# The inverse product over 32 places with a row's high and low part stacked in one operand, and the correction added a stage later

## The chip, the cores and the metric

One NeuronCore of a Trainium2 chip runs the whole kernel in one launch. The metric is device time in microseconds (us), the median over several executions.

## The reference, cut to what matters

```
x: (1, 2048, 576)    w_r, w_i: (2048, 289)    w_gate, w_up: (576, 4608)    w_down: (4608, 576)
xn = layernorm(x)                                     # over the 576
spectral = irfft2(rfft2(xn) * (w_r + 1j * w_i))       # over rows (2048) and columns (576)
glu = (sigmoid(xn @ w_gate) * (xn @ w_up)) @ w_down
out = x + spectral + glu
```

Everything is float32.

## The kernel before, in words

**Precision.** A product of float32 matrices is made on TensorE from rounded parts. Each operand is split into a high part (a copy on ScalarE that rounds) and a low part (the operand minus its high part, on VectorE), and three products are added: high by high, low by high, high by low.

**The gated unit.** The hidden dimension of 4608 is cut into 36 blocks, and the 2048 rows into two halves of two blocks each. A block of hidden columns is a unit. In most units the 2 × 2 block products are made by a scheme of seven products instead of eight (`unit`, with `prod` at L659: seven matmuls of 512 columns on a product bank, called pA, pB or pE). The down product is also done by seven rounds (`seven`, matmuls at L1016, 12 of 288 columns into a pair of banks called ps), and its last part plainly (`down`, L809, po). The units of the second pass over the rows take about 2.8 us per step, seven steps each. Weights for these units lie in one buffer `w_6086`, which SP refills slot by slot after TensorE has read a slot.

**The spectral part.** The 2048-point transform along the rows is split into 64 × 32. Phase 1 does the transform over the columns and the forward product over the 64 places, phase 2 does the forward product over the 32 places, the multiplication with the filter and the inverse product over the 32 places, phase 3 does the inverse product over the 64 places and the inverse column transform. Each phase is a generator per chunk of rows (16 chunks, `phase1b`, `phase2`, `phase3`), and every `yield` ends a chunk of work. After each step of the gated unit `aside` advances every live generator by one chunk. `U1`, `U2`, `U3` (L51) give each phase its first step and the steps between two generators, so the spectral work is spread under the gated unit by these numbers. A scheduler then orders the instructions of each engine when the program is built, and an engine runs them in that order. All but a few DMAs are issued by SP in one queue, in order.

**Phase 2 before (L496 to L541).** Per i: x2 (580 KB) and the filter piece ri (580 KB, two buffers) are loaded. Two products pb0 and pb1 (L513, two matmuls of 290 columns each) use stacked operands: the high part of the data in 64 partitions, the low part in the other 64, and main and correction come out in two halves of the bank and are added on VectorE (L517). s is turned with four copies on ScalarE (sw, L522), multiplied with the filter (L523 to L527), and z, which holds two sets of 32 complex places in its 128 partitions (real above imaginary, 64 rows a set), is split into zh (ScalarE, L530) and zl (VectorE, L532). The inverse product pc (L538) is six matmuls: for each of two column groups high, low and correction, with a 128 × 128 block-diagonal constant. ScalarE copies pc to u (L540), and one DMA (L541, 290 KB) writes u to the scratch array `sc2` in HBM.

**Phase 3 before (L544 to L612).** Per t: u (290 KB) and constants ai are loaded, u is split into uh (L559) and ul (L560), the product py follows (L566, six matmuls), its result is copied to y (L569) and the remainder columns split into rp (L572, L573). pz (L579, L582) are six transposes into one pair of banks, z3h, z3r and z3l (L587 to L589) are their split copies, pe (L599) twelve matmuls, and L601 to L610 add the result to `fin` or `acc`. All pairs of banks (pb, pc, ps, py, pz, pe, po) come from one pool of two pairs.

Of the kernel before, what the change touches and what calls it, by code (L numbers as in the profile page):

```python
# [167 lines left out]
def spectral_glu_kernel(ctx: ExitStack, tc: tile.TileContext, x, xt, xg, ri, w_in, w_down, out):  # L168
# [327 lines left out]
    def phase2(i):  # L496
        pool, bm, zz = R["pool"], R["bm"], R["zz"]
        kl = 2 * i
# [10 lines left out]
        for h, o in enumerate((s, c)):  # L509
            yield  # L510
            pb = pair(f"pb{i}_{h}")
            for j in range(2):
                nc.tensor.matmul(pb[:, j, :NQ], bm[:, h, :], x2[:, h, j, :], start=True, stop=True)  # L513
# [16 lines left out]
        nc.scalar.activation(zh, z, AF.Copy)  # L530
        yield
        nc.vector.tensor_tensor(zl, z, f32(zh), op=OP.subtract)  # L532
        yield
        yield
        pc = pair(f"pc{i}")
        for j in range(2):
            for n, (k, m) in enumerate(((2, zh), (2, zl), (3, zh))):
                nc.tensor.matmul(pc[:, j, :NQ], bm[:, k, :], m[:, j, :], start=n == 0, stop=n == 2)  # L538
# [1 line left out]
        nc.scalar.activation(u, pc[:, :, :NQ], AF.Copy)  # L540
        nc.sync.dma_start(sc2.rearrange("(p kl) n -> p kl n", kl=N2)[:, kl:kl + 2], u)  # L541

    def phase3(t):
        pool, di, dr = R["pool"], R["di"], R["dr"]  # L544
# [15 lines left out]
        nc.vector.tensor_tensor(ul, u, f32(uh), op=OP.subtract)  # L560
# [3 lines left out]
        for sl in range(2):  # L564
            for n, (h, m) in enumerate(((0, uh), (0, ul), (1, uh))):
                nc.tensor.matmul(py[:, sl, :NQ], ai[:, sl, h, :], m[:, sl, :], start=n == 0, stop=n == 2)  # L566
# [985 lines left out]
```

## Time and profile before

| | us |
|---|---|
| median of 3 executions | 1357.94 (1357.67 to 1358.01) |
| profiled execution | 1357.6 |
| its span, first to last instruction | 1355.8 |
| TensorE busy | 1344.5 (99%) |
| VectorE busy | 1078.5 (80%) |
| ScalarE busy | 815.3 (60%) |
| granted TensorE clock | 1.00 throughout |

The profile names PE for TensorE's matmuls, PEld for its weight loads, DVE for VectorE, ACT for ScalarE, SP for SyncE, and SPq for its DMA queue. `out<-in` are the names of tiles; a line such as L538 is that line of the kernel. Busy shares are means over stages with different limits, and the chain of work that ended last says which engine's work sets the end.

### The profile page before, as it was taken

The page shows a single profiled execution, that of the slowest core. Times are in us where ns is not written, and L with a number is a line of the kernel's source. Part 1 is how long each engine was busy: PE and PEld are TensorE (multiplying, and loading weights), DVE is VectorE, ACT ScalarE, POOL GpSimd, SP SyncE. Part 2 cuts the span into 40 slices and gives each one's busy share as a digit, 9 for nine tenths or more (in the row PEclk, how much of TensorE's full clock was granted, in tenths as well). Part 3 has the DMA queues.
Part 4 walks back from the last instruction along what each step waited for, and adds up shares of the span by engine and source line. Part 5 has one row for each costly group of instructions (what it writes and reads, how often), then busy time and mean ns, then how long its engine had stood idle before and what let it go on. Part 6 is the DMA issues. An engine that isn't in the chain of part 4 may idle for free.

```text
span 1355.8 us, 20569 instructions
## 1 busy us (share of the span) xinstructions
PE 1344.5 (99%) x7589; PEld 1193.7 (88%) x7589; DVE 1078.5 (80%) x1624; ACT 815.3 (60%) x1266; POOL 3.3 (0%) x5
## 2 busy tenths in 40 slices
PE   8999999999999999999999999999999999999998
PEld 6888888888888888889899999988888889889997
DVE  7898998889898897888477777758878856777786
ACT  6667777776767677778355554546767634444432
POOL 0000000000000000000000000000000000000000
PEclk9999999999999999999999999999999999999999
DMA  6468888778787877688899887798999787776543
GB/s 235 187 256 324 313 314 309 285 287 330 283 326 290 321 290 285 265 313 293 287 336 294 259 263 251 209 310 308 307 304 313 244 280 252 237 228 207 187 135 88
DMA packets 151828, 366.17 MB, mean 270 GB/s; under 512 B 14240, under 2 KB 54704, under 8 KB 147120
## 3 DMA queue, kind: packets, MB, share of 16 engines
q1 hardware_dynamic: 150736, 363.55, 77.4%
q8 instruction: 60, 0.98, 0.3%
q10 hardware_dynamic: 992, 1.31, 0.3%
q14 instruction: 40, 0.33, 0.1%
HBM read 217.82 MB, written 146.98 MB: 269 GB/s over the span
## 4 chain that ended last, share of the span: by engine, by line
PE 93%; DVE 4%; issue 1%; ACT 1%; DMA 0%; SPq 0%; DVEq 0%; ACTq 0%
PE ps L1016 27%; PE pB L659 24%; PE pE L659 16%; PE pA L659 16%; PE pd L475 2%; PE po L809 2%; PE pe L599 1%; PE pa L490 1%; PE pc L538 1%; PE py L566 1%; PE pb L513 1%; PE pz L579 0%; DVE w L287 0%; DMA acc<-in_x 0%; PE pg L659 0%
## 5 line engine op out<-in xcount | busy, mean ns | idle before, releaser
L1016 PE MATMUL ps<-wf,hs 128*128 128x288 f32 x2856 | 419.7, 296 | 0.0
L1016 PEld LDWEIGHTS ps<-wf,hs 128*128 128x128 f32 x2856 | 400.9, 188 | 16.8 <-ACT u L540 1.6
L659 PE MATMUL pB<-X,w 128*128 128x512 f32 x1477 | 373.0, 391 | 0.0
L659 PEld LDWEIGHTS pB<-X,w 128*128 128x128 f32 x1477 | 270.0, 188 | 49.2 <-DVE w L287 0.7
L659 PE MATMUL pE<-X,w 128*128 128x512 f32 x1050 | 262.0, 391 | 0.7 <-DVE ys L782 0.7
L659 PE MATMUL pA<-X,w 128*128 128x512 f32 (+1 forms) x1020 | 255.9, 389 | 0.6 <-ACT X L424 0.5
L659 PEld LDWEIGHTS pE<-X,w 128*128 128x128 f32 x1050 | 191.7, 188 | 35.7 <-DVE ys L782 0.9
L659 PEld LDWEIGHTS pA<-X,w 128*128 128x128 f32 x1020 | 185.3, 188 | 33.6 <-ACT X L424 0.9
L939 DVE TENSOR_TENSOR hs<-ys,hs 128x1024 fp32r<-128x1024 f32 x119 | 145.4, 1222 | 37.7 <-ACT hs L936 36.4
L936 ACT ACTIVATE hs<-ys 128x1024 fp32r<-128x1024 f32 x119 | 125.7, 1056 | 55.5 <-PE ps L1016 30.8
L285 ACT ACTIVATE w<-raw 128x768 fp32r<-128x768 f32 (+1 forms) x106 | 100.3, 948 | 25.4 <-DVE raw L312 10.0
L287 DVE TENSOR_TENSOR w<-raw,w 128x512 fp32r<-128x512 f32 (+1 forms) x106 | 81.8, 771 | 7.3 <-ACT w L285 7.2
L784 DVE TENSOR_TENSOR ys<-ys,g 128x1024 f32<-128x1024 f32 x68 | 83.2, 1223 | 3.5 <-ACT u L540 0.5
L932 DVE TENSOR_TENSOR ys<-ys 128x1024 f32<-128x1024 f32 x68 | 83.0, 1221 | 0.6
L765 ACT ACTIVATE g<-pB 128x512 f32<-128x512 f32 x69 | 41.2, 597 | 63.5 <-PE pB L659 63.2
L751 ACT ACTIVATE v<-pB 128x512 f32<-128x512 f32 x69 | 41.2, 596 | 51.5 <-PE pB L659 44.7
L782 DVE TENSOR_TENSOR ys<-v,pE 128x512 f32<-128x512 f32 x68 | 46.5, 684 | 26.2 <-PE pE L659 25.4
L762 DVE TENSOR_TENSOR ys<-v,pE 128x512 f32<-128x512 f32 x69 | 47.2, 684 | 24.1 <-ACT v L757 23.5
L998 ACT ACTIVATE qs<-ps 128x576 f32<-128x576 f32 x54 | 35.1, 651 | 48.3 <-PE ps L1016 47.6
L952 DVE TENSOR_TENSOR acc<-acc,ps 128x576 f32<-128x576 f32 x57 | 42.7, 750 | 24.6 <-PE ps L1016 24.3
L952 DVE TENSOR_TENSOR qs<-qs,ps 128x576 f32<-128x576 f32 x64 | 48.1, 752 | 15.3 <-PE ps L1016 14.4
L757 ACT ACTIVATE v<-pB 128x512 f32<-128x512 f32 x69 | 40.9, 593 | 31.7 <-PE pB L659 31.7
(179 smaller groups left out, 1482.5 us busy)
## 6 DMA issues: line engine op xcount, KB each, us to landing
w<-wsp SPq DMA_DIRECT2D x249, 320.0 KB, 4.1
wsp<-w SPq DMA_DIRECT2D x34, 2240.0 KB, 7.1
fsp<-wf SPq DMA_DIRECT2D x126, 288.0 KB, 4.1
wf<-fsp SPq DMA_DIRECT2D x112, 288.0 KB, 4.3
raw<-in_w SPq DMA_DIRECT2D x34, 768.0 KB, 6.0
dt<-in_wd SPq DMA_DIRECT2D x36, 288.0 KB, 5.4
x<-sc SPq DMA_DIRECT2D x16, 580.0 KB, 5.6
ri<-in_ri SPq DMA_DIRECT2D x16, 580.0 KB, 5.7
```

Of the source, the lines that this page charges most:

```text
L285: placed(nc.scalar.activation(o[:, :, :3, :], src, AF.Copy))
L287: placed(nc.vector.tensor_tensor(o[:, :, 3:, :], src[:, :, :KT, :], f32(o[:, :, :KT, :]), op=OP.subtract))
L659: (tc.keep_in_program_order if pinned and j == 0 else strictly)(nc.tensor.matmul(bank[:, cols], w[:, sw, :], X[:, x, sx, cols], start=star ...
L751: nc.scalar.activation(v[:, 0], bank["B"], AF.Copy)
L762: nc.vector.tensor_tensor(y1, v[:, 1], bank["E"], op=OP.add)
L782: nc.vector.tensor_tensor(place(u, 0), v[:, 0], bank["E"], op=OP.add)
L784: nc.vector.tensor_tensor(h, h, g, op=OP.mult)
L932: nc.vector.tensor_tensor(o, at(a), at(b), op=op)
L936: nc.scalar.activation(hs[:, :, 0], o, AF.Copy)
L939: nc.vector.tensor_tensor(hs[:, :, 1], o, f32(hs[:, :, 0]), op=OP.subtract)
L952: nc.vector.tensor_tensor(o, a, b, op=op)
L1016: nc.tensor.matmul(pd[:, s], h[:, g, a, m], w[:, g, b], start=q == 0 and not seeded, stop=q == len(parts_) - 1, skip_group_check=seeded)
```

## The change

- The inverse product gets the form that the forward product has. One tile zz holds, in its first slot, the high part of z's first 64 partitions with their low part in the other 64, and in its second slot the high part of z's last 64 partitions with their low part in the first 64. It is filled by two ScalarE copies and two VectorE subtracts, each over 64 partitions. A chunk now has two products pc_0 and pc_1 of two matmuls each, one chunk apart, with constants that are stacked likewise (the host's constants). The main sum comes out in 64 partitions and the correction in the other 64.
- They aren't added here. Each of the two is copied to u and written by its own DMA, so `sc2` has two planes, main and correction.
- Phase 3 loads both (u with two buffers, v with one), adds them on VectorE (v = u + v, in chunk 4 after the loads in chunk 0), splits v, and writes the low part back into u.
- The four rows of places that a chunk of phase 2 takes now lie one behind the other in the scratch arrays, so x2 is one run per partition (the host lays out the filter to match); the filter piece has one buffer and is asked for in the chunk of pb0; chunks within phase 2 are moved, and phase 3 begins at step 156 instead of 153, a new t every 4.15 steps instead of 4.4 (two chunks longer each).

```
-U1, U2, U3 = (2, 4.1), (78, 4.1), (153, 4.4)
+U1, U2, U3 = (2, 4.1), (78, 4.1), (156, 4.15)
...
-    b = np.stack([np.block([[bh, bl], [bh, none]]), np.block([[bl, bh], [none, bh]]), *_split(bi)], 1)
+    b = np.stack([np.block(v) for v in ([[bh, bl], [bh, none]], [[bl, bh], [none, bh]], [[ih, il], [ih, none]], [[ih, none], [ih, il]])], 1)
...
-    sc2 = tc.dram_tile([N2 * P, NQ], F32, name="sc2")
+    sc2 = tc.dram_tile([2, N2 * P, NQ], F32, name="sc2")
...
     def phase2(i):
...
-        x2 = pool.tile([P, 2, 2, NQ], F32R, tag="x2", name=f"x2{i}", bufs=2)
-        nc.sync.dma_start(f32(x2), sc1.rearrange("a (q h kl) n -> (a q) h kl n", h=2, kl=N2)[:, :, kl:kl + 2])
-        w = pool.tile([P, 2, 2, NQ], F32, tag="ri", name=f"ri{i}", bufs=2)
-        nc.sync.dma_start(w.rearrange("p a j n -> p (a j n)"), ri[i])
-        wr, wi = w[:, 0], w[:, 1]
-        yield
+        x2 = pool.tile([P, 4, NQ], F32R, tag="x2", name=f"x2{i}", bufs=2)
+        nc.sync.dma_start(f32(x2), sc1.rearrange("a (q k) n -> (a q) k n", k=N1)[:, 4 * i:4 * i + 4])
...
             nc.scalar.activation(o, pb[:, :, :NQ], AF.Copy)
+            if h == 0:
+                w = pool.tile([P, 2, 2, NQ], F32, tag="ri", name=f"ri{i}", bufs=1)
+                nc.sync.dma_start(w.rearrange("p a j n -> p (a j n)"), ri[i])
+                wr, wi = w[:, 0], w[:, 1]
...
-        zh, zl = zz[i % len(zz)]
-        nc.scalar.activation(zh, z, AF.Copy)
-        yield
-        nc.vector.tensor_tensor(zl, z, f32(zh), op=OP.subtract)
-        yield
-        yield
-        pc = pair(f"pc{i}")
+        yield
+        yield
+        for h in range(2):
+            nc.scalar.activation(zz[half[h], h], z[half[h]], AF.Copy)
+        yield
+        for h in range(2):
+            nc.vector.tensor_tensor(zz[half[1 - h], h], z[half[h]], f32(zz[half[h], h]), op=OP.subtract)
+        yield
         for j in range(2):
-            for n, (k, m) in enumerate(((2, zh), (2, zl), (3, zh))):
-                nc.tensor.matmul(pc[:, j, :NQ], bm[:, k, :], m[:, j, :], start=n == 0, stop=n == 2)
-        u = pool.tile([P, 2, NQ], F32, tag="u", name=f"u{i}", bufs=2)
-        nc.scalar.activation(u, pc[:, :, :NQ], AF.Copy)
-        nc.sync.dma_start(sc2.rearrange("(p kl) n -> p kl n", kl=N2)[:, kl:kl + 2], u)
+            yield
+            pc = pair(f"pc{i}_{j}")
+            for h in range(2):
+                nc.tensor.matmul(pc[:, h, :NQ], bm[:, 2 + h, :], zz[:, h, j, :], start=True, stop=True)
+            u = pool.tile([P, 2, NQ], F32, tag="u", name=f"u{i}_{j}", bufs=2)
+            nc.scalar.activation(u, pc[:, :, :NQ], AF.Copy)
+            nc.sync.dma_start(sc2.rearrange("a (q k) n -> (a q) k n", k=N1)[:, 4 * i + 2 * j:4 * i + 2 * j + 2], u)
...
     def phase3(t):
...
-        u = pool.tile([P, 2, NQ], F32, tag="u3", name=f"u3{t}", bufs=2)
-        nc.sync.dma_start(u, sc2[2 * t * P:(2 * t + 2) * P].rearrange("(j p) n -> p j n", j=2))
+        u = pool.tile([P, 2, NQ], F32R, tag="u3", name=f"u3{t}", bufs=2)
+        v = pool.tile([P, 2, NQ], F32, tag="v3", name=f"v3{t}")
+        for a, o in enumerate((f32(u), v)):
+            nc.sync.dma_start(o, sc2[a, 2 * t * P:(2 * t + 2) * P].rearrange("(j p) n -> p j n", j=2))
...
+        yield
+        nc.vector.tensor_tensor(v, f32(u), v, op=OP.add)
+        yield
         uh = pool.tile([P, 2, NQ], F32R, tag="uh", name=f"uh{t}")
-        ul = pool.tile([P, 2, NQ], F32R, tag="ul", name=f"ul{t}")
-        tc.keep_in_program_order(nc.scalar.activation(uh, u, AF.Copy))
-        nc.vector.tensor_tensor(ul, u, f32(uh), op=OP.subtract)
+        tc.keep_in_program_order(nc.scalar.activation(uh, v, AF.Copy))
+        nc.vector.tensor_tensor(u, v, f32(uh), op=OP.subtract)
...
-            for n, (h, m) in enumerate(((0, uh), (0, ul), (1, uh))):
+            for n, (h, m) in enumerate(((0, uh), (0, u), (1, uh))):
```

**How the order moves.** Three places are shown, each before and after; a row is a line of code, an operation, its result and operands, and its shape, with xN where it is repeated. Numbers at the end of names only tell one buffer from another, and lines after L496 are shifted by a few in the changed kernel.

First, TensorE in one period of the second stage, before:

```order
L659 MATMUL pA_8941<-X,w_6086 128x512 x7
L538 MATMUL pc_8950<-zh,bmt 128x290
L538 MATMUL pc_8950<-zl,bmt 128x290
L538 MATMUL pc_8950<-zh,bmt 128x290 x2
L538 MATMUL pc_8950<-zl,bmt 128x290
L538 MATMUL pc_8950<-zh,bmt 128x290
L513 MATMUL pb_0_8962<-x_8858,bmt 128x290 x2
L659 MATMUL pE_8831<-X,w_6086 128x512 x3
L1016 MATMUL ps_6_1_0_8939<-wf_6_1_8761,hs_6_1_8877 128x288 x12
L659 MATMUL pB_8830<-X,w_6086 128x512 x7
L513 MATMUL pb_1_8999<-x_8858,bmt 128x290 x2
```

The same engine and place after (L661 is the block's line now, L506 pb, L1018 ps):

```order
L661 MATMUL pB_8837<-X,w_6086 128x512 x7
L538 MATMUL pc_0_8995<-zz,bmt 128x290 x2
L661 MATMUL pE_8838<-X,w_6086 128x512 x7
L538 MATMUL pc_1_9012<-zz,bmt 128x290 x2
L1018 MATMUL ps_6_1_1_9003<-wf_6_1_8762,hs_6_1_8870 128x288 x12
L661 MATMUL pE_9047<-X,w_6086 128x512 x7
L506 MATMUL pb_0_9062<-x_8965,bmt 128x290 x2
L661 MATMUL pB_9046<-X,w_6086 128x512 x7
L506 MATMUL pb_1_9078<-x_8965,bmt 128x290 x2
L1018 MATMUL ps_6_2_0_9068<-wf_6_2_8867,hs_6_2_8983 128x288 x12
```

The six inverse matmuls and the pb_0 that followed them are four groups of two, each behind a whole block, and ps stands directly behind pc_1.

Second, VectorE in one period of the third stage, before (ev, fin: the final adds of an earlier t; qs: the sums of the seven rounds; ys, hs: the gated unit):

```order
L560 TENSOR_TENSOR ul_11567<-u_11473,uh_11566 128x580
L952 TENSOR_TENSOR qs<-qs,ps_12_3_0_11538 128x576
L606 TENSOR_TENSOR ev_11563<-ev_11563 128x2x144
L608 TENSOR_TENSOR fin_11343<-fin_11343,ev_11563 128x576
L782 TENSOR_TENSOR ys<-v_11382,pE_11384 128x512
L610 TENSOR_TENSOR fin_11343<-fin_11343,ev_11563 128x288 x2
L784 TENSOR_TENSOR ys<-ys,g_11381 128x2x512
L573 TENSOR_TENSOR rp_11627<-py_11618,rp_11627 128x2x34
```

After, the same place (v_11398 and v_11580 are in the single buffer of phase 3, v_11421 and g_11420 belong to the gated unit):

```order
L564 TENSOR_TENSOR u_11397<-v_11398,uh_11576 128x580
L610 TENSOR_TENSOR ev_11573<-ev_11573 128x2x144
L612 TENSOR_TENSOR fin_11272<-fin_11272,ev_11573 128x576
L954 TENSOR_TENSOR qs<-qs,ps_12_3_0_11587 128x576
L614 TENSOR_TENSOR fin_11272<-fin_11272,ev_11573 128x288 x2
L784 TENSOR_TENSOR ys<-v_11421,pE_11423 128x512
L560 TENSOR_TENSOR v_11580<-u_11579,v_11580 128x580
L577 TENSOR_TENSOR rp_11638<-py_11629,rp_11638 128x2x34
L786 TENSOR_TENSOR ys<-ys,g_11420 128x2x512
```

The add of the next t (L560) stands between the low-part subtract of this t (L564) and its remainder subtract (L577).

Third, TensorE at the last t of phase 3, before:

```order
L579 MATMUL pz_12926<-idf,y_12896 128x2x64 x4
L582 MATMUL pz_12926<-idr,rp_12898 102x2x64 x2
L659 MATMUL pB_12838<-X,w_6086 128x512 x7
L599 MATMUL pe_12951<-dit,z3h_12933 128x288
L599 MATMUL pe_12951<-drt,z3r_12935 128x288
L599 MATMUL pe_12951<-dit,z3h_12933 128x144 x2
L599 MATMUL pe_12951<-dit,z3l_12934 128x144 x2
```

And after (L811 is the down product):

```order
L583 MATMUL pz_13033<-idf,y_13016 128x2x64 x4
L586 MATMUL pz_13033<-idr,rp_13018 102x2x64 x2
L811 MATMUL po_11_A<-wb_17_0_12886,hp_17_0_13006 128x288 x3
L603 MATMUL pe_13047<-dit,z3h_13040 128x288
L661 MATMUL pE_12909<-X,w_6086 128x512
L603 MATMUL pe_13047<-drt,z3r_13042 128x288
L603 MATMUL pe_13047<-dit,z3h_13040 128x144 x2
L661 MATMUL pE_12909<-X,w_6086 128x512
L603 MATMUL pe_13047<-dit,z3l_13041 128x144 x2
```

Between pz and pe there are three short matmuls where a block of seven long ones stood.

More of the change, by code (lines that the diff above doesn't have):

```diff
@@ L110, in _constants @@
     bh, bl = (v.reshape(2, N2, N1).transpose(1, 0, 2).reshape(N1, N1) for v in _split(_cplx(np.exp(-1j * ph))))
+    ih, il = (v.reshape(N1, 2, N2).transpose(0, 2, 1).reshape(N1, N1) for v in _split(_cplx(np.exp(1j * ph))))
     none = np.zeros_like(bl)
-    bi = _cplx(np.kron(np.exp(1j * ph), np.eye(2)))
-    at = np.arange(P).reshape(2, N2, 2)
-    bi = bi[at.transpose(2, 0, 1).ravel()][:, at.transpose(1, 0, 2).ravel()]
-    b = np.stack([np.block([[bh, bl], [bh, none]]), np.block([[bl, bh], [none, bh]]), *_split(bi)], 1)
+    b = np.stack([np.block(v) for v in ([[bh, bl], [bh, none]], [[bl, bh], [none, bh]], [[ih, il], [ih, none]], [[ih, none], [ih, il]])], 1)
     out["bm"] = b.reshape(P, 4 * P)
@@ L148, in _layout @@
     w = w[[1, 1, 0, 0], [0, 1, 1, 0]].reshape(4, KT + 1, P, NF, P).transpose(3, 2, 0, 1, 4)
-    v = np.stack([w_r, w_i])[:, :, KOF].reshape(2, N2, 2, N2 // 2, 2, NQ).transpose(3, 2, 1, 0, 4, 5)
+    v = np.stack([w_r, w_i])[:, :, KOF].reshape(2, N2, N2 // 2, 2, 2, NQ).transpose(2, 4, 1, 0, 3, 5)
     v = np.broadcast_to(v[:, :, None], (N2 // 2, 2, 2, N2, 2, 2, NQ))
@@ L497, in phase2 @@
         pool, bm, zz = R["pool"], R["bm"], R["zz"]
-        kl = 2 * i
-        x2 = pool.tile([P, 2, 2, NQ], F32R, tag="x2", name=f"x2{i}", bufs=2)
-        nc.sync.dma_start(f32(x2), sc1.rearrange("a (q h kl) n -> (a q) h kl n", h=2, kl=N2)[:, :, kl:kl + 2])
-        w = pool.tile([P, 2, 2, NQ], F32, tag="ri", name=f"ri{i}", bufs=2)
-        nc.sync.dma_start(w.rearrange("p a j n -> p (a j n)"), ri[i])
-        wr, wi = w[:, 0], w[:, 1]
-        yield
+        x2 = pool.tile([P, 4, NQ], F32R, tag="x2", name=f"x2{i}", bufs=2)
+        nc.sync.dma_start(f32(x2), sc1.rearrange("a (q k) n -> (a q) k n", k=N1)[:, 4 * i:4 * i + 4])
         yield
@@ L512, in phase2 @@
             for j in range(2):
-                nc.tensor.matmul(pb[:, j, :NQ], bm[:, h, :], x2[:, h, j, :], start=True, stop=True)
+                nc.tensor.matmul(pb[:, j, :NQ], bm[:, h, :], x2[:, 2 * j + h, :], start=True, stop=True)
             nc.scalar.activation(o, pb[:, :, :NQ], AF.Copy)
+            if h == 0:
+                w = pool.tile([P, 2, 2, NQ], F32, tag="ri", name=f"ri{i}", bufs=1)
+                nc.sync.dma_start(w.rearrange("p a j n -> p (a j n)"), ri[i])
+                wr, wi = w[:, 0], w[:, 1]
         yield
@@ L522, in phase2 @@
             nc.scalar.activation(sw[o], s[v], AF.Copy, scale=-1.0 if k % 2 == 0 else 1.0)
-        z = pool.tile([P, 2, NQ], F32, tag="z", name=f"z{i}")
+        z = pool.tile([P, 2, NQ], F32, tag="z", name=f"z{i}", bufs=2)
         nc.vector.tensor_tensor(z, wr, s, op=OP.mult)
@@ L623, in stage2 @@
         load_r(bm, con["bm"].rearrange("p (k m) -> p k m", k=4))
-        zh = pool.tile([P, 2, NQ], F32R, name="zh")
-        zl = pool.tile([P, 2, NQ], F32R, name="zl")
-        R["zz"] = [(zh, zl)]
+        R["zz"] = pool.tile([P, 2, 2, NQ], F32R, name="zz")
         yield
```

## Prediction

> **What bounds the kernel now.** I read the page first, for busy shares and the chain that ended last, then the stretches of time, then the chain inside the stretch that the change touches, and last the waits.
>
> ```profile
> PE 1344.5 (99%) x7589; PEld 1193.7 (88%) x7589; DVE 1078.5 (80%) x1624; ACT 815.3 (60%) x1266; POOL 3.3 (0%) x5
> ...
> PE 93%; DVE 4%; issue 1%; ACT 1%; DMA 0%; SPq 0%; DVEq 0%; ACTq 0%
> ```
>
> TensorE is busy 99% of the span and makes 93% of the chain. An average hides stages, so here are stretches: start:end, their length, then busy time (instructions) of PE, PEld, DVE, ACT and POOL, the granted clock, the DMA share, GB/s. The third stage's generators run in 1100 to 1330, the second's in about 903 to 1093; the last three rows are for comparison.
>
> ```profile
> 903.00:1056.00 153.00, 153.00 (x862) 135.66 (x861) 124.14 (x157) 107.24 (x164) 0.00 (x0) 1.00 0.90 306
> 903.00:1093.00 190.00, 190.00 (x1073) 168.83 (x1072) 151.50 (x190) 128.68 (x197) 0.00 (x0) 1.00 0.87 290
> 1100.00:1330.00 230.00, 229.23 (x1399) 207.46 (x1398) 167.12 (x251) 98.12 (x166) 0.00 (x0) 1.00 0.65 209
> 1100.00:1110.00 10.00, 10.00 (x58) 8.90 (x57) 5.23 (x6) 4.63 (x8) 0.00 (x0) 1.00 1.02 372
> 890.00:900.00 10.00, 10.00 (x57) 8.91 (x57) 3.61 (x5) 2.86 (x4) 0.00 (x0) 1.00 0.99 347
> 200.00:300.00 100.00, 99.32 (x544) 87.68 (x544) 89.51 (x147) 70.90 (x106) 0.00 (x0) 1.00 0.75 282
> ```
>
> In the second stage PE has no gap at all, at full clock. In the third it loses 0.77 us of 230. So a matmul taken out of the second stage shortens the kernel by its own length, and a wait put in front of PE lengthens it by its own length, since what stands behind PE has no slack to give back. The chain inside one second-stage period shows the size of a matmul (start, length, line, how many):
>
> ```profile
> 946.29 0.80 PE pc L538 x6
> 947.09 0.27 PE pb L513 x2
> ...
> 950.64 0.27 PE pb L513 x2
> 950.90 1.62 PE pB L659 x7
> 952.52 1.61 PE ps L1016 x12
> 954.14 1.59 PE pA L659 x7
> 955.73 1.59 PE pB L659 x7
> 957.32 0.80 PE pc L538 x6
> ```
>
> A period lasts 957.32 − 946.29 = 11.03 us, of which the six inverse matmuls take 0.80, or 0.133 each. A block right behind an insertion takes 1.61 to 1.62, one behind another block 1.59.
>
> **The change part by part.** *Matmuls removed.* Six of 290 columns become two and two for each of 16 chunks: 96 becomes 64. 32 × 0.133 = **−4.3 us**, all on PE's path. The Trainium skill, page "TensorE: Matmul & The Clock Gate", section "Back-to-back issue gap", gives the gap of an isolated warm matmul as its columns divided by 2.4 GHz, plus 2.5 ns; for 290 columns that is an estimate of 0.123 us and −3.9 us for the 32. The chain's 0.133 is larger, and the measurement decides.
>
> *The same blocks in a new order (stage 2).* The four remaining matmuls stand at two places of a step instead of one, so 16 more insertions cut the row of blocks. At 0.01 to 0.03 us each (1.62 and 1.61 against 1.59) that is at most +0.5. Each pair of product banks must also be emptied by ACT before the next pair uses it (us waited, times, longest):
>
> ```profile
> PEld ps L1016 <- ACT u L540: 1.6, 7, 0.3
> PEld pz L582 <- DVE rp L573: 1.0, 1, 1.0
> ```
>
> Today the weight load of the seventh-round product waits for u seven times, 1.6 us in all, 0.3 at the longest, and PE hides it. After, the product behind pc_1 takes the pair of pc_0, which ACT has had one block and two matmuls to empty: 1.59 + 0.27 = 1.86 us, against 0.66 for the copy plus whatever ACT is in. Sign scalings of 4 × 0.69 can stand in front of it. Bounds: −0.8 us (if half of the 1.6 is PE's after all, and goes) to +1.6 (16 × 0.1). I take **0**, nearest to the row that shows PE without a gap.
>
> *More work on ACT and DVE.* Group rows for the stage, with busy time and mean ns of one:
>
> ```profile
> L522 ACT ACTIVATE sw<-s 32x580 f32<-32x580 f32 x64 | 44.0, 687 | 14.6 <-DVE s L517 13.8
> ...
> L532 DVE TENSOR_TENSOR zl<-z,zh 128x580 fp32r<-128x580 f32 x16 | 12.2, 760 | 2.1 <-ACT zh L530 0.8
> ...
> L530 ACT ACTIVATE zh<-z 128x580 fp32r<-128x580 f32 x16 | 11.0, 687 | 0.5 <-DVE z L527 0.4
> L540 ACT ACTIVATE u<-pc 128x580 f32<-128x580 f32 x16 | 10.5, 656 | 19.5 <-PE pc L538 19.5
> ```
>
> The 32-partition copy takes as long as the 128-partition one, 687 ns, so half a tile costs a whole one. ACT gets 16 more copies for zz (16 × 0.687) and 16 more for u (16 × 0.656): 21.5 us. DVE gets 16 × 0.760 = 12.2. ACT's share of 903 to 1093 rises from 128.7 to 150.2 of about 187 (80%), DVE's from 151.5 to 163.7 (88%). DVE stood at 89.5% in 200 to 300 with PE losing 0.7 of 100 us. All of it is hidden under PE: z is complete in chunk 7 and multiplied in 13 and 14, where it was 8 and 12. Without that cover a late half would cost up to 0.7 us in a chunk. **0**, with up to +1.
>
> *DMA.* 16 more writes of 290 KB in stage 2, 16 more loads in stage 3, all on SP's one queue, which also refills the single weight buffer slot by slot. The step's other loads stay the same bytes (x2 in longer runs, ri one place later in a single buffer, asked for when the previous product with wi has read it, one chunk ahead of use). Stage 2 then moves 306 × 153 = 46.8 MB plus 14 × 0.297 = 51.0 MB in about 151 us: 338 GB/s, a share of 0.99. PE kept going without a gap at 1.02 and 372 GB/s, and at 0.99 and 347. **0** forecast; the rival prices the other case. Stage 3, at 0.65, has room.
>
> *The third stage's sum.* Here a wait is new. v has one buffer. The load of v(t+1) waits on SP for the low-part subtract of t; behind it, on DVE's queue, the add u+v of t+1 stands directly in front of the small remainder subtract rp(t); and PE's transposes pz(t) wait for rp(t). What stands in the add's place today, at one of the places where only one block separates py and pz, and at another where py comes later behind the subtract:
>
> ```profile
> 1117.95 0.76 DVE L560 TENSOR_TENSOR ul<-u,uh 128x580 fp32r<-128x580 f32 x1
> ...
> 1120.59 0.29 PE L566 MATMUL py<-uh,ai 128*128 128x290 f32 x1
> ...
> 1146.40 0.76 DVE L560 TENSOR_TENSOR ul<-u,uh 128x580 fp32r<-128x580 f32 x1
> ...
> 1148.65 0.29 PE L566 MATMUL py<-uh,ai 128*128 128x290 f32 x1
> ...
> 1150.51 0.23 DVE L573 TENSOR_TENSOR rp<-py,rp 128x68 fp32r<-128x68 f32 x1 [2.09 <-ACT rp L572]
> ...
> 1151.42 0.36 PE L582 MATMUL pz<-idr,rp 128*102 128x128 f32 x2
> ```
>
> From the subtract's end (1147.16) to pz (1151.42) there are 4.26 us; the add (0.76) and rp (0.23) take 0.99, so a load may take 3.27 from its release. With the distance from subtract to py of the first place (1.88 instead of 1.49) it is 3.66. How long such a load takes, of the same tile shape in the same stage:
>
> ```profile
> DMA to landing us min/median/max: 2.7/3.6/5.6
> ```
>
> So at the median PE waits 0 to 0.3 us in a period with the short gap. The new order has some seven such periods; the others have a product and a block between py and pz, about 2 us more, which covers the add. I take 3.75 for the load (above the median, the queue being fuller) and 3.5 for the room: 7 × 0.25 = **+1.8 us**. Bounds: 0 (landing at 3.27 or less) to +6.3 (three of the seven at the longest landing, 3 × (5.6 − 3.5)). The one old wait of the weight load at pz, 1.0 us in the row above, may go or stay; it is inside these bounds. The add itself (16 × 0.76) is otherwise hidden, DVE being at 73% of that stretch.
>
> *The end.* The last period starts one step sooner but lasts two chunks more, so its final steps come closer to the last rounds. Today:
>
> ```profile
> 1331.15 0.36 PE L582 MATMUL pz<-idr,rp 128*102 128x128 f32 x2
> ...
> 1331.55 0.60 ACT L587 ACTIVATE z3h<-pz 128x512 fp32r<-128x512 f32 x1
> ...
> 1333.03 0.29 PE L599 MATMUL pe<-dit,z3h 128*128 128x288 f32 x1
> ```
>
> A block of 1.6 us stands between pz's end (1331.51) and pe, which needs z3h, ready at 1332.15, 0.64 after pz. After, three short products (3 × 0.13 = 0.4) stand there: a wait of about 0.25 to 0.45, and perhaps as much again where the first product of round 17's other half comes ahead of its ACT copy of 0.63. **+0.7**, bounds 0 and +1.4.
>
> **The sum.** −4.3 + 0 + 0 + 0 + 1.8 + 0.7 = −1.8 us, on the profiled execution's 1357.6 (span 1355.8): **1355.8**. That execution lies 0.3 us below the median of the runs shown, 1357.94; forecast and chances are against 1357.94, from which 0.2% is 2.7 us, about what a measurement of this kernel can tell from no change.
>
> **The rivals.**
> (A) *The gain stands whole*: the v loads land within 3.3 us and the end finds cover. For it: SP's 32 queued loads of stage 3 run at a share of 0.65. Against it: the median 3.6. Time 1357.6 − 4.3 = 1353.3. Chance 0.28.
> (B) *Slower: the single v buffer decides the third stage.* With a fuller queue a load takes 4.6 us from its release, and DVE is held at the add, ahead of rp and of what PE's blocks need from DVE behind it: seven short periods at 4.6 − 3.5 = 1.1 are 7.7 us, less 4.3 and plus 0.7, is +4.1: 1361.7. It decides from 3.5 + (4.3 − 0.7)/7 = 4.0 us per load. For it: the maximum 5.6 and the second-stage share. Against: stage 3's DMA share. Chance 0.15.
> (C) *DMA fills up in stage 2.* If 338 GB/s cannot be held, weight refills come late and PE waits about what the transfers exceed: at 320 GB/s the 51.0 MB take 159 us, 8 more than 151; refills asked for early hide some of it, and I price half, +4, on the forecast or on (A): 1359.8 or 1357.3. For it: share 0.99. Against: 372 in ten undisturbed microseconds. Chance 0.07. The Trainium skill, page "DMA: Bandwidth & Descriptors", section "Specifications", puts HBM's limit for one core near 358 GB/s; by that figure the need of 338 just fits, though the row with 372 is above it.
>
> **How the numbers follow.** The forecast case has 0.50, its own range 1353.8 to 1357.4 (its terms' nearer bounds). From 1357.94, faster by over 0.2% means below 1355.2: all of (A), 0.28, and about a fifth of the forecast case, 0.11: 0.39. Slower by over 0.2% means above 1360.7: about 0.10 of (B), 0.03 of (C): 0.13. The rest, 0.48, lies within. For eight in ten the range runs from 1352.7, (A) with 0.6 of the old bank waits gone too, to 1360.2, into (B) and past (C).
>
> **What would show each step.** Right: pc ×64 at about 0.13 us each, in pairs; no PE time lost between 903 and 1093; waits of PE at pz for rp, with DVE waiting at the add for the load of v, about 0.25 us in some seven periods; a short wait of pe for z3h near the end. Wrong: no wait at pz at all (then A), waits of 1 us there (B), or PE waiting for w in stage 2 at a DMA share of 1 (C). If ACT or DVE hold PE in stage 2 (waits of ps for u, of pc for zz), my zero for that part failed.

## The result and the profile after

The changed kernel takes 1360.27 us (1359.6 to 1361.52, 17 runs) against 1357.79 for the kernel before (17 runs): a ratio of 1.0018, 95% interval 1.0012 to 1.0025. It is 2.5 us slower where 1355.8 was forecast, and 0.07 us above the range. In the profiled execution the span is 1358.7, 2.9 us more than before.

The page of the changed kernel shows where to look: PE is still busy 99%, but the chain that ended last now runs through VectorE and ScalarE for 9% instead of 5%, and names of stage 2 (sw, zz, s) are in it.

```profile
PE 1343.7 (99%) x7557; PEld 1189.9 (88%) x7557; DVE 1104.9 (81%) x1656; ACT 835.4 (61%) x1298; POOL 3.3 (0%) x5
...
PE 88%; DVE 6%; ACT 3%; issue 1%; DMA 1%; DVEq 0%; SPq 0%; ACTq 0%
PE ps L1018 26%; PE pB L661 22%; PE pE L661 16%; PE pA L661 15%; PE pd L473 2%; PE po L811 2%; PE pe L603 1%; PE pa L488 1%; ACT sw L519 1%; DVE zz L532 1%; PE py L570 1%; DVE s L514 1%; DVE hs L941 1%; ACT hs L938 1%; DVE ys L934 1%
```

The stretches of before, in the trace of after (PE, PEld, DVE, ACT, POOL, clock, DMA share, GB/s): PE has gaps of 1.28 us in 903 to 1056 and of 2.10 in 903 to 1093, where it had none, and of 1.88 instead of 0.77 in stage 3. VectorE's busy time in the first stretch rose from 124.1 to 135.7 (89%), ScalarE's from 107.2 to 122.8. DMA stands at 0.91 with 317 GB/s, not at the 338 that I worked out.

```profile
903.00:1056.00 153.00, 151.72 (x845) 134.17 (x844) 135.67 (x170) 122.76 (x188) 0.00 (x0) 1.00 0.91 317
903.00:1093.00 190.00, 187.90 (x1041) 165.75 (x1040) 166.32 (x207) 147.36 (x226) 0.00 (x0) 1.00 0.91 315
...
1100.00:1330.00 230.00, 228.12 (x1386) 205.44 (x1385) 177.38 (x264) 96.98 (x163) 0.00 (x0) 1.00 0.73 232
```

To put the 2.9 us into stages I use instructions that both kernels have in the same place of the gated unit: the block pB just ahead of stage 2, and a seventh-round product behind the last pc and ahead of the first py. TensorE's rows in the timeline, before:

```profile
900.66 1.75 PE L659 MATMUL pB<-X,w 128*128 128x512 f32 x7
...
1103.20 1.75 PE L1016 MATMUL ps<-wf,hs 128*128 128x288 f32 x12
```

and after:

```profile
900.57 1.75 PE L661 MATMUL pB<-X,w 128*128 128x512 f32 x7
...
1102.79 1.75 PE L1018 MATMUL ps<-wf,hs 128*128 128x288 f32 x12
```

Between the two, before took 202.54 us and after 202.22: **stage 2 gained 0.3 us** where 32 matmuls of 0.133, 4.27 us, are gone. So it lost 3.95 elsewhere. From the second landmark to the end the changed kernel is 2.9 + 0.4 = **3.3 us worse**. The waits of PE from 895 us on, after (us, times, longest; before there was one of 0.7, at pz):

```profile
PE pz L586 <- DVE rp L577: 1.3, 2, 0.7
PE ps L1018 <- ACT s L507: 1.0, 3, 0.5
PE ps L1018 <- ACT u L540: 0.9, 2, 0.5
PE po_A L811 <- ACT hp L845: 0.5, 1, 0.5
PE ps L1018 <- DVE acc L954: 0.4, 1, 0.4
PE pe L603 <- ACT z3h L591: 0.2, 1, 0.2
```

In TensorE's timeline six of the stage's seven gaps, 2.0 of the 2.1 us, stand at a seventh-round product (ps) directly behind a pc. The gaps are only about half of the loss. Here is one of 0.52 us:

```profile
1005.53 0.42 PE L538 MATMUL pc<-zz,bmt 128*128 128x290 f32 x2
1006.47 1.88 PE L1018 MATMUL ps<-wf,hs 128*128 128x288 f32 x12 [0.52 <-ACT u L540]
```

The product starts 0.94 us after pc, where 0.27 is usual (1092.67 to 1092.94), and the block behind it starts 1.72 us later (at 1008.19), where 1.58 is usual (1102.79 to 1104.37). So this wait costs about 0.8 us. Summed from start to start in the same way, the six places cost 3.6 of the 3.95 us.

One of these waits, followed back along the chain (start, length, engine, result, line). VectorE works through eight operations without a gap; the sum s, which the sign copies need, comes behind both subtracts of zz; ScalarE then has a sign copy (939.29) and a copy for the gated unit, and only then the copy u of pc_0, whose banks the product at 941.20 reuses:

```profile
932.83 0.76 DVE zz L532
...
933.61 0.77 DVE zz L532
...
934.40 0.76 DVE z L524
935.16 0.60 DVE ys L764
...
935.79 0.77 DVE s L514
...
936.58 1.23 DVE hs L941
937.81 0.66 DVE acc L954
...
938.50 0.77 DVE s L514
...
940.01 0.60 ACT g L767
940.61 0.55 ACT u L540
...
941.20 0.91 PE ps L1018 x5
```

### The profile page after: what moved, and what is told of

The parts are those of the page before. It is cut to its first block, busy times and chain, and to the rows that moved or that the text cites. A ratio compares the mean times of both kernels' runs of the same rounds, so it can differ in the third digit from the quotient of the medians.

```text
span 1358.7 us, 20614 instructions
## 1 busy us (share of the span) xinstructions
PE 1343.7 (99%) x7557; PEld 1189.9 (88%) x7557; DVE 1104.9 (81%) x1656; ACT 835.4 (61%) x1298; POOL 3.3 (0%) x5
## 4 chain that ended last, share of the span: by engine, by line
PE 88%; DVE 6%; ACT 3%; issue 1%; DMA 1%; DVEq 0%; SPq 0%; ACTq 0%
PE ps L1018 26%; PE pB L661 22%; PE pE L661 16%; PE pA L661 15%; PE pd L473 2%; PE po L811 2%; PE pe L603 1%; PE pa L488 1%; ACT sw L519 1%; DVE zz L532 1%; PE py L570 1%; DVE s L514 1%; DVE hs L941 1%; ACT hs L938 1%; DVE ys L934 1%
## 5 line engine op out<-in xcount | busy, mean ns | idle before, releaser
L1018 PE MATMUL ps<-wf,hs 128*128 128x288 f32 x2856 | 420.3, 296 | 2.5 <-ACT s L507 1.0
L1018 PEld LDWEIGHTS ps<-wf,hs 128*128 128x128 f32 x2856 | 400.4, 188 | 18.6 <-ACT u L540 1.7
L661 PE MATMUL pB<-X,w 128*128 128x512 f32 x1477 | 372.3, 391 | 0.0
L661 PEld LDWEIGHTS pB<-X,w 128*128 128x128 f32 x1477 | 269.8, 188 | 49.2 <-DVE w L285 0.7
L661 PE MATMUL pE<-X,w 128*128 128x512 f32 x1050 | 262.5, 391 | 0.7 <-DVE ys L784 0.7
L661 PE MATMUL pA<-X,w 128*128 128x512 f32 (+1 forms) x1020 | 256.0, 389 | 0.5 <-ACT X L422 0.2
L661 PEld LDWEIGHTS pE<-X,w 128*128 128x128 f32 x1050 | 191.3, 188 | 35.4 <-DVE ys L784 0.9
L661 PEld LDWEIGHTS pA<-X,w 128*128 128x128 f32 x1020 | 184.9, 188 | 33.8 <-ACT X L422 0.7
L941 DVE TENSOR_TENSOR hs<-ys,hs 128x1024 fp32r<-128x1024 f32 x119 | 145.3, 1221 | 39.4 <-ACT hs L938 38.0
L753 ACT ACTIVATE v<-pB 128x512 f32<-128x512 f32 x69 | 41.1, 596 | 46.0 <-PE pB L661 45.8
L756 ACT ACTIVATE g<-pA 128x512 f32<-128x512 f32 x69 | 41.0, 594 | 30.0 <-PE pA L661 29.6
```

The lines of the kernel that those rows point to most:

```text
L661: (tc.keep_in_program_order if pinned and j == 0 else strictly)(nc.tensor.matmul(bank[:, cols], w[:, sw, :], X[:, x, sx, cols], start=star ...
L753: nc.scalar.activation(v[:, 0], bank["B"], AF.Copy)
L941: nc.vector.tensor_tensor(hs[:, :, 1], o, f32(hs[:, :, 0]), op=OP.subtract)
L1018: nc.tensor.matmul(pd[:, s], h[:, g, a, m], w[:, g, b], start=q == 0 and not seeded, stop=q == len(parts_) - 1, skip_group_check=seeded)
```

## The experiments

For each run the change against the profile of before is split at the same two landmarks, one profiled execution each: "stage 2" from pB to the seventh-round product, "later" from there to the end of the span. A single profile is not exact: the changed kernel and the eight others with its code for phase 3 (a_full, a_lo1, a_hi1, a_pcm1, p_212, v_212, a_pool, a_p2_41) show +2.6 to +3.3 there. Medians are of all runs of that kernel; the kernel before, run beside them, had 1357.65 to 1357.79.

| run | median us | ratio, 95% interval | stage 2 | later |
|---|---|---|---|---|
| changed kernel | 1360.27 | 1.0018 (1.0012 to 1.0025) | −0.3 | +3.3 |
| a_full | 1356.57 | 0.9995 (0.9985 to 1.0004) | −4.1 | +2.6 |
| a_lo1 | 1357.35 | 0.9997 (0.9988 to 1.0006) | −2.8 | +2.7 |
| a_hi1 | 1360.66 | 1.0021 (1.0012 to 1.0030) | 0.0 | +3.2 |
| b_halves | 1358.01 | 1.0002 (0.9993 to 1.0012) | +0.3 | +0.1 |
| b_all | 1358.68 | 1.0007 (0.9998 to 1.0016) | +1.0 | 0.0 |
| b_three | 1359.33 | 1.0011 (1.0002 to 1.0020) | +1.5 | 0.0 |
| a_pcm1 | 1360.58 | 1.0022 (1.0011 to 1.0033) | −0.6 | +2.7 |
| p_212 | 1360.84 | 1.0025 (1.0015 to 1.0035) | −0.1 | +3.1 |
| v_212 | 1364.88 | 1.0055 (1.0040 to 1.0070) | +4.6 | +2.8 |
| a_pool | 1362.62 | 1.0036 (1.0023 to 1.0049) | +1.6 | +2.7 |
| a_p2_41 | 1360.42 | 1.0021 (1.0011 to 1.0031) | 0.0 | +2.8 |
| a_s4_41 | 1365.57 | 1.0054 (1.0037 to 1.0070) | +4.9 | +3.1 |
| a_v2 | 1367.08 | 1.0065 (1.0050 to 1.0080) | −0.3 | +10.1 |
| a_vpool | 1360.33 | 1.0019 (1.0009 to 1.0028) | −0.3 | +2.8 |
| a_v0 | 1359.57 | 1.0014 (1.0004 to 1.0023) | −0.2 | +1.9 |
| b_u3 | 1359.40 | 1.0013 (1.0004 to 1.0022) | 0.0 | +1.6 |
| u_41 | 1359.74 | 1.0013 (1.0004 to 1.0022) | −0.2 | +1.9 |
| p_212_41 | 1359.93 | 1.0017 (1.0007 to 1.0026) | +0.1 | +2.1 |

After seeing the result my theory was: the extra work of VectorE and ScalarE makes the copies of pc late ("load"). The rivals: it is the place of that copy in ScalarE's queue ("queue"), or the 1.86 us between pc_0 and the reuse of its banks ("turn").

### Less work on both engines

```
-        for h in range(2):
-            nc.scalar.activation(zz[half[h], h], z[half[h]], AF.Copy)
+        nc.scalar.activation(zz[:, 0], z, AF.Copy)
...
-        for h in range(2):
-            nc.vector.tensor_tensor(zz[half[1 - h], h], z[half[h]], f32(zz[half[h], h]), op=OP.subtract)
+        nc.vector.tensor_tensor(zz[:, 1], z, f32(zz[:, 0]), op=OP.subtract)
```

> The changed kernel with zz's high parts made by one copy over all 128 partitions instead of two over 64, and its low parts by one subtract instead of two; everything else, pairs of banks and transfers included, as in the changed kernel. It leaves half of each product's operand out of place, so what it writes is not the reference's output; it is run for its time. It takes 16 copies (11.0 us) from ScalarE and 16 subtracts (12.2 us) from VectorE in stage 2. The changed kernel ran at 1360.3 and lost 3.2 us in stage 2 where the seventh-round product stands right behind pc_1 and waits for the copy of pc_0. Theory load (the extra work on the two engines makes that copy late): the waits fall to under 1 us, time 1357.5 to 1358.3. Theory queue (the copy stands behind four sign copies that wait for sums on VectorE, whatever the load): half of the waits stay, 1358.7 to 1359.3. Theory turn (1.86 us from pc_0 to the reuse of its banks is too short in itself): no gain, 1360.

Measured: 1356.57, lower than any theory had it. PE's gap in the first stretch is 0.01 us and stage 2 gives 4.1 of the 4.27 us. With the order of the products, the banks and all transfers as in the changed kernel, the turn alone costs 0.2 us at most.

```profile
903.00:1056.00 153.00, 152.99 (x857) 136.01 (x856) 128.61 (x161) 116.08 (x179) 0.00 (x0) 1.00 0.93 322
```

### One engine at a time

a_hi1 keeps the two subtracts and has one full copy, a_lo1 the reverse. Both fill zz once at the start of the stage, since part of it is then never written.

```
-        for h in range(2):
-            nc.scalar.activation(zz[half[h], h], z[half[h]], AF.Copy)
+        nc.scalar.activation(zz[:, 0], z, AF.Copy)
```

> The changed kernel with one full-width ScalarE copy for zz's high parts in place of two half ones, and the two half subtracts of VectorE kept: 11.0 us less on ScalarE in stage 2, nothing less on VectorE. It leaves the second set's high part out of place, so the output is not the reference's. With both engines relieved the time was 1356.6 and stage 2's waits were gone; in the changed kernel it is 1360.3 with 3.2 us of waits. If ScalarE's load is what makes the copies of pc late: 1356.8 to 1357.5, waits under 0.7. If it is VectorE's (the sums of s come late, and ScalarE's sign copies with them): 1359.3 to 1360.2, waits of 2 us or more.

> The reverse: two half copies on ScalarE, one full-width subtract on VectorE in place of two half ones, 12.2 us less on VectorE in stage 2. It leaves the second set's low part out of place, so the output is not the reference's. If VectorE's load decides: 1356.8 to 1357.5, waits under 0.7. If ScalarE's: 1359.3 to 1360.2. If both are needed for the waits to arise, both of these kernels lie near 1357.

Measured: 1360.66 and 1357.35. ScalarE's 11 us less bring nothing while VectorE has both subtracts; VectorE's 12.2 us less bring 2.9 us of time, and stage 2 gains 2.8 instead of 0.3. With that, ScalarE's copies bring the other 1.3 (a_full against a_lo1). In the same stretch VectorE's column goes with PE's, not ScalarE's. a_hi1:

```profile
903.00:1056.00 153.00, 151.47 (x841) 133.85 (x840) 135.73 (x169) 114.31 (x176) 0.00 (x0) 1.00 0.91 316
```

a_lo1:

```profile
903.00:1056.00 153.00, 152.73 (x854) 135.62 (x853) 128.03 (x159) 123.44 (x190) 0.00 (x0) 1.00 0.93 320
```

### The same work in the kernel before

```
-        nc.scalar.activation(zh, z, AF.Copy)
+        for o in half:
+            nc.scalar.activation(zh[o], z[o], AF.Copy)
...
-        nc.vector.tensor_tensor(zl, z, f32(zh), op=OP.subtract)
+        for o in half:
+            nc.vector.tensor_tensor(zl[o], z[o], f32(zh[o]), op=OP.subtract)
```

> The kernel before with zh and zl made in two halves of 64 partitions each, so that ScalarE gets 16 more copies (11 us) and VectorE 16 more subtracts (12.2 us) in stage 2, and nothing else moves. Theory load: PE begins to wait in stage 2, by 1 to 3 us, time 1359 to 1361. Theories queue and turn: the copy of pc is not behind the sign copies here and its banks are not reused by a product right behind a second pc, so no loss, 1357.8 within 0.5.

b_three makes zl alone in pieces of 64, 32 and 32 partitions. b_all is b_halves with a second copy of pc and a second write.

```
+        u2 = pool.tile([P, 2, NQ], F32, tag="u", name=f"w{i}", bufs=2)
+        nc.scalar.activation(u2, pc[:, :, :NQ], AF.Copy)
+        nc.sync.dma_start(sc2b.rearrange("(p kl) n -> p kl n", kl=N2)[:, kl:kl + 2], u2)
```

> The kernel before with zl made in three pieces (64, 32 and 32 partitions): two more subtracts of some 0.76 us for each of 16 chunks, so VectorE is busier in 903 to 1056 than in the changed kernel (about 124 + 20 = 144 of 153 us, where the changed kernel has 135.7), with the banks, copies and transfers of before. If the amount of work on VectorE alone decides: waits of 3 us or more, 1360.5 to 1362. If it hurts only together with two products in a row, each with its own copy ahead of the next product: 1357.8 to 1358.8.

> The kernel before with all the second stage's extra work of the changed one, but none of its new order or timing: zh and zl in halves, the copy of pc made a second time into a second u, and a second write of 290 KB to a second plane that nobody reads. 16 copies and 16 more copies on ScalarE, 16 subtracts on VectorE, 16 writes. If the amount of work on both engines decides: the changed kernel's stage-2 loss of some 3.5 us, 1360.5 to 1361.5. If VectorE's amount decides only where two products with a copy each stand in a row ahead of the seventh-round product (the new order): 1357.8 to 1359.

Measured: 1358.01, 1359.33 and 1358.68. Work on VectorE does cost time in the old order too, but less: with VectorE at 141.1 of 153 us (b_three) PE has gaps of 0.22 us and stage 2 loses 1.5, where the changed kernel at 135.7 loses 3.95. All of the extra work, writes included (b_all), loses 1.0 in the old order. The rows of b_three and b_all:

```profile
903.00:1056.00 153.00, 152.78 (x857) 134.69 (x856) 141.14 (x179) 106.20 (x161) 0.00 (x0) 1.00 0.90 300
...
903.00:1056.00 153.00, 152.95 (x858) 134.75 (x857) 132.12 (x167) 120.80 (x185) 0.00 (x0) 1.00 0.94 321
```

So neither the amount alone (1.0 us in the old order) nor the new order alone (0.2 us in a_full, which still has the second copy u and its write) makes the loss; the two together do.

### Other places for the same work

a_pcm1 drops one chunk boundary ahead of pc_0. v_212 makes zz's parts one chunk earlier; p_212 does so with two buffers for zz and one for z.

```
-        yield
         for j in range(2):
             yield
             pc = pair(f"pc{i}_{j}")
```

> The changed kernel with one chunk boundary less between zz's low parts and pc_0, so pc_0 and pc_1 come one step earlier. The load on every engine is unchanged. On ScalarE the copy of pc_0 then stands ahead of the sign copies of a later chunk for most chunks, and on TensorE pc_0 is followed by pb_1, three matmuls of a block and the product that reuses pc_0's banks: 0.27 + 0.68 = 0.95 us instead of 1.86. Theory queue: waits of the product for u fall from 3.2 us to under 1.5, time 1358 to 1359. Theory turn: less room, waits grow, 1361 or more. Theory load: no change, 1360.3 within 0.5.

> The changed kernel, complete, with zz's high and low parts one chunk earlier (chunks 9 and 10 instead of 10 and 11), pc_0 and pc_1 where they were. The work on every engine is the same. On VectorE the two subtracts then stand behind the next chunk's sums and ahead of its product with wi, where VectorE waited 5 us for ScalarE's sign copies, instead of ahead of the sums. If the place of the two subtracts in VectorE's queue decides (ahead of the sums that ScalarE's sign copies wait for): waits in stage 2 fall under 1.5 us, 1357.3 to 1358.8. If only the amount of work counts: 1360 to 1361.

> The changed kernel, complete, with two buffers for zz, one for z, and zz's parts made one chunk earlier (9 and 10), with nothing of the next chunk in their way; TensorE's order is that of the changed kernel. The same work, and the two subtracts in other places of VectorE's queue. If the place ahead of the sums decides: stage 2's waits under 1.5 us, 1357.5 to 1359. If the amount of work next to this order of products does: 1360 to 1361.

Measured: 1360.58, 1364.88, 1360.84. In a_pcm1 PE's waits for u are gone, as the queue theory had it, but a wait of a block for ys (0.6 us), of pb for a sum, and of pc for zz stand in their place: the lateness only shows elsewhere. On the time the theories queue (1358 to 1359) and turn (1361 or more) both miss, and load (1360.3 within 0.5) holds. In v_212 the next chunk's high parts come ahead of pc_1 in the program, so that pc_1's weight load waits for them (11 times, 6.3 us) and pc_1 multiplies them instead of its own; its 4.6 us tell nothing about the place. p_212 has no such clash, and with the subtracts in that place stage 2 is as before (−0.1 against −0.3).

### Moving work off VectorE

a_pool puts z = wr × s on GpSimd; a_p2_41 one of the two low-part subtracts (in spite of its name its phase 3 keeps the changed kernel's pace); a_s4_41 has four half copies of pb_0 and pb_1 and one full add for two half ones.

```
-        nc.vector.tensor_tensor(z, wr, s, op=OP.mult)
+        nc.gpsimd.tensor_tensor(z, wr, s, op=OP.mult)
```

> The changed kernel, complete, with the product of the filter's real part and s (z, 16 times 128x580) on GpSimd, which does nothing in stage 2, instead of VectorE: 12.1 us less on VectorE, and its queue is one entry shorter ahead of the sums of the next chunk. Its result is needed only at the add of z and sw, some 3 us later. If VectorE's load decides and GpSimd is done within 3 us without slowing VectorE: 1356.8 to 1357.8. If the two slow each other down or ScalarE decides: 1359.5 to 1361.

> The changed kernel, complete, with one of the two low-part subtracts of a chunk on GpSimd: 12.1 us less on VectorE as in the kernel with one full subtract, which ran at 1357.4. The subtract has two chunks, some 5 us, until its product, and about 1.6 us is to be expected for it on GpSimd. If VectorE's amount decides and GpSimd does not slow it: 1357.2 to 1358. If VectorE's operations become longer beside GpSimd's (they took 3 to 8% longer in the run with z there): 1359 to 1361.

```
-            nc.scalar.activation(o, pb[:, :, :NQ], AF.Copy)
+            nc.scalar.activation(s[half[h]], pb[half[h], :, :NQ], AF.Copy)
+            nc.scalar.activation(c[half[h]], pb[half[1 - h], :, :NQ], AF.Copy)
...
-        for h, o in enumerate((s, c)):
-            nc.vector.tensor_tensor(s[half[h]], o[half[h]], o[half[1 - h]], op=OP.add)
+        nc.vector.tensor_tensor(s, s, c, op=OP.add)
```

> The changed kernel, complete, with VectorE's work of a chunk cut by one operation at ScalarE's cost: pb_0 and pb_1 are copied in four half copies, so that main parts and corrections lie in two tiles of 128 partitions and one add (0.76 us) takes the place of two; and a new t of phase 3 every 4.1 steps. VectorE 12 us less, ScalarE 21 us more (some 140 of 153 us). If VectorE's amount alone decides: stage 2 as in the kernel with one full subtract, end as before: 1356.3 to 1357.5. If ScalarE at 90% has become the bound: 1360 or more.

Measured: 1362.62, 1360.42 and 1365.57: no cure in any of them. On GpSimd the product takes 1.57 us instead of 0.76, and VectorE's own operations grow beside it (zz from 757 to 785 ns, ys from 1221 to 1323). In a_p2_41 they grow so much (the zz that stays from 757 to 952 ns, the add of z from 759 to 901) that VectorE's busy time in 903 to 1093 falls by 1.9 us only, from 166.3 to 164.4. In a_pool it does fall, in the first stretch to as little as in a_lo1, and yet PE's gaps grow to 2.32 us; which wait does that was not taken apart. Its row:

```profile
903.00:1056.00 153.00, 150.68 (x833) 132.49 (x832) 127.22 (x153) 120.86 (x186) 22.24 (x14) 1.00 0.91 315
```

In a_s4_41 VectorE falls to 119.6 of 153 us and PE still loses 4.6 there, since now the banks of pb wait for two copies. Its stretch:

```profile
903.00:1056.00 153.00, 148.38 (x812) 129.22 (x811) 119.58 (x150) 136.05 (x208) 0.00 (x0) 1.00 0.89 308
```

The waits:

```profile
PE ps L1018 <- ACT s L508: 4.0, 5, 1.2
PE ps L1018 <- ACT u L540: 0.9, 2, 0.5
```

Here it is ScalarE's copies of a pair of banks that come late, with VectorE at 78%. A low share of one engine is thus no cure by itself, as a_pool shows too: TensorE waits for the copy that frees its banks, and other things than VectorE's load can make that copy late.

### The third stage and the end

```
-        v = pool.tile([P, 2, NQ], F32, tag="v3", name=f"v3{t}")
+        v = pool.tile([P, 2, NQ], F32, tag="v3", name=f"v3{t}", bufs=2)
```

> The changed kernel with two buffers for v; to make room the constants ai of phase 3 have one buffer and are asked for behind the add instead of at the start. Takes away the wait of v's load for the low part of the previous t. If the single buffer costs the third stage what was forecast (1.8 us): 1358.5 to 1359.3. Rival: in the trace of the changed kernel only one of the waits for rp (0.8 us at 1123) has v's load ahead of it, and loads landed in 3.0 us at the median, so 0.8 or less: 1359.5 to 1360.2.

```
-        nc.vector.tensor_tensor(v, f32(u), v, op=OP.add)
+        nc.gpsimd.tensor_tensor(v, f32(u), v, op=OP.add)
```

> The changed kernel, complete, with phase 3's add of u and v on GpSimd instead of VectorE, so that the wait for the load of v no longer stands in VectorE's queue ahead of rp. If the single buffer of v works as forecast, by way of that queue, for 1 to 1.8 us: 1358.5 to 1359.4. If the extra loss of stage 3 has other reasons (the pace of one t in 4.15 steps, the chunks' new neighbours): 1360 or more.

> The changed kernel without the loads of v: the add takes a constant that is there already in its place, so the correction of the inverse product is left out (and a constant added), and the 16 loads and every wait for them are gone. The add is still made. If the loads of v cost stage 3 its 1 to 1.8 us: 1358.4 to 1359.4. If the pace of phase 3 and its neighbours do: 1360 to 1360.5.

b_u3 is the kernel before with `U3 = (156, 4.15)` and two more `yield`s ahead of uh; u_41 the changed kernel with `U3 = (156, 4.1)`.

> The kernel before with phase 3 alone in the new time: first step 156, a new t every 4.15 steps, two chunks longer. No second load, no add, no stacked product. In the changed kernel stage 3 lost 2.0 us more than before and the end 1.2 us more. If both come of the new pace: 1360.5 to 1361.2. If stage 3's loss is v's load and add: 1358.8 to 1359.3, from the end alone.

> The changed kernel, complete, with phase 3 beginning a new t every 4.1 steps instead of 4.15, so that the last one begins a step sooner and the order of TensorE at the end is that of the kernel before again (a whole block between pz and pe, and the last rounds in one piece). The end lost 1.2 us more than before in the changed kernel. If the late last t is the reason: 1359.0 to 1359.5. If not, 1360.3 within 0.4.

> As the kernel with two buffers for zz and its parts a chunk earlier, with a new t of phase 3 every 4.1 steps as well, which took the 1.2 us of the end away in the profile. If the two add up: 0.5 to 1.2 us below that kernel; if its stage 2 is cured, 1356.5 to 1358, the complete version that would beat before.

Measured: 1367.08, 1360.33, 1359.57, 1359.40, 1359.74 and 1359.93. The 3.3 us come apart so: the new pace and the late last t alone, in the kernel before, cost 1.6 (b_u3); with the add but no loads of v it is 1.9 (a_v0); the loads are the rest, 1.4, or 0.7 if it is 2.6, as in a_full. The medians say much the same: b_u3 lies 1.7 above its kernel before, a_v0 0.7 below the changed kernel. With the last t a step sooner (u_41) PE's waits at the end are gone and the later part falls to +1.9; the median falls by 0.5 only, so that single profile flatters it. p_212_41 lies 0.9 below p_212. a_v0 and u_41 fell between the two times that were expected, and b_u3 0.1 above the nearer one. The add on GpSimd is no help: the new wait of pz for rp is gone, but pe waits 0.5 us for z3l. a_v2 missed by 7 us to the other side: with a second buffer for v, VectorE waited at the add for the load of u instead, 13.1 us in all, and pe then waited for z3l.

```profile
DVE v L558 <- DMA u<-sc: 13.1, 12, 2.6
```

Why u came late there (its load, ai's or their new places in SP's queue) was not taken apart, so this run says nothing about v's single buffer. No complete version of the change ran below the kernel before.

## Why the prediction was wrong

**The removed matmuls: right.** a_full gives 4.1 of 4.27 us in stage 2 once both engines are relieved.

**The step that failed: "All of it is hidden under PE ... 0, with up to +1", and the 0 for the copies of u.** Together they were given at most +1.6 and +1, and +3.95 was measured. The sign that was named for this failure is the one that came: ps waits for u, and for s. The share itself was well worked out (166.3 of 190 us is 88%), but I compared it with a stretch where 89.5% had gone with PE losing 0.7 of 100 us, 200 to 300, which has none of phase 2's operations. In stage 2 VectorE's sums feed ScalarE's sign copies, these stand ahead of the copies that free the banks, and the next product needs the banks at once; in a row of operations without a gap, as the one ahead of 941.20, both subtracts delay the sum behind them. a_lo1 shows that VectorE's added subtracts decide (2.5 of 3.95 go with them), a_full that ScalarE's copies are the next 1.3, b_all that the same work in the old order costs 1.0. That the new order multiplies the loss follows from these together; which neighbours in it do so stays open, since an earlier pc (a_pcm1) and an earlier zz (p_212) left the loss as it was, and work taken off VectorE in other places (a_pool, a_p2_41) did not lessen it.

**DMA: right to leave at 0.** No wait of PE for w was found. The first stretch moved 317 GB/s at a share of 0.91, not 338. Over 903 to 1093 the rate rose from 290 to 315 GB/s, which is the 4.75 MB of the 16 writes, so some of the traffic lies later than I put it.

**The third stage: the size fits, the mechanism does so in part.** +1.8 was forecast; the later part has 3.3, of which the end is about 1.3 and this stage 2.0. The forecast wait exists. This is the chain at 1117.68, with the longest landing of all, 5.1 us, where PE waits 0.6 to 0.7 at pz:

```profile
1116.89 0.77 DVE u L564
...
1117.68 5.13 DMA v<-sc
...
1122.89 0.06 DVE v L560
...
1123.58 0.23 DVE rp L577
```

But it was the only such wait of pz that is new, not seven of 0.25: the other one in the rows above, 0.7, is in the kernel before too. The loads landed sooner than the 3.75 us that I took, in 3.0 at the median, though VectorE waited for them ten times:

```profile
DVE v L560 <- DMA v<-sc: 6.9, 10, 1.5
```

The landing of its 16 loads:

```profile
DMA to landing us min/median/max: 2.6/3.0/5.1
```

Two terms were missing. The add, which I had hidden, stands in VectorE's row ahead of the sum acc for which ps waits 0.4 us at 1256; that wait is there without any load of v too (a_v0, 0.5), and not in b_u3, which has no add. And the pace of phase 3 gives about 0.3 (1.6 in b_u3 less 1.3 at the end), as the add does (1.9 in a_v0 less 1.6), though differences so small are within what single profiles vary by.

**The end: mechanism right, mis-sized.** +0.7 (to 1.4) was forecast. Both waits came where they were put, pe for z3h and po_A for hp, 0.7 us in the rows of PE's waits above. As in stage 2 (3.6 us for gaps of 2.0 at six places) each costs some 0.26 us more than its gap, so the end lost 1.2 to 1.3. u_41's order takes that away in its profile, but its median shows only 0.5. One of the waits in the timeline of after:

```profile
1334.35 0.36 PE L586 MATMUL pz<-idr,rp 128*102 128x128 f32 x2
...
1334.75 0.60 ACT L591 ACTIVATE z3h<-pz 128x512 fp32r<-128x512 f32 x1
...
1335.40 0.40 PE L603 MATMUL pe<-dit,z3h 128*128 128x288 f32 x1 [0.23 <-ACT z3h L591]
```

**The rivals.** (A), the whole gain, was not reached by any run: a_full has its stage 2, −4.1, but not its third stage and end. (B) had the right sign for the wrong reason. The case that came, VectorE's queue as the bound of stage 2, was not among them: it stood in the text as a bound of +1 us instead.

## What to carry to other kernels

An engine at 81% of a stage is no free cover for another 8%: read which of its operations a copy of PSUM banks waits for, and whether the next product takes those banks at once. Here 12.2 us more on VectorE cost TensorE 2.5 us in such a place, while in the old order 23 us more (b_three, 903 to 1093) cost 1.5. Half a tile costs a whole operation (64x580 took 687 ns on ScalarE and 757 on VectorE, 128x580 687 and 760), so stacking by halves must be paid with twice the operations, and matmuls saved on one side should be weighed against that sum on the engine whose queue has no gaps. A pipeline made two chunks longer also costs at its end, and that is cheap to try with the step numbers alone.

## What the hardware showed beyond that

GpSimd's product of two 128x580 float32 tiles took 1570 ns, VectorE's 758, and VectorE's operation of 1024 elements went from 1221 to 1323 ns beside it (GpSimd's spans are rough in these profiles). VectorE's group of the changed kernel, in 903 to 1093:

```profile
L934 DVE TENSOR_TENSOR ys<-ys 128x1024 f32<-128x1024 f32 x11 | 13.4, 1221 | 0.2
```

The same group in a_pool:

```profile
L934 DVE TENSOR_TENSOR ys<-ys 128x1024 f32<-128x1024 f32 x11 | 14.6, 1323 | 0.2
```

GpSimd's row there:

```profile
L521 POOL TENSOR_TENSOR z<-ri,s 128x580 f32<-128x580 f32 x16 | 25.1, 1570 | 1048.1 <-DVE s L514 1048.1
```

The Trainium skill, page "GPSIMD Engine Reference", section "Specifications", says that GpSimd's access to SBUF is shared with VectorE and contended by VectorE instructions with two SBUF inputs; the longer operations of VectorE in this run agree with that. All that grew read two tiles in SBUF (ys, hs, zz, sw), while the sums that read PSUM stayed at 749 to 750 ns (qs, acc).
